# A second read moved beside the scores, one weight conversion held back, one weight split moved up

## The chip, the cores and the metric

The kernel runs on one core of one Trainium2 chip. The core has five engines that run their own instruction lists and wait for each other by semaphores: TensorE (PE in the profile), VectorE (DVE), ScalarE (ACT), GpSimd (POOL) and SyncE (SP). The metric is the device time of one execution in microseconds (us); the kernel before took 1189.47 us (median of three runs, 1189.44 to 1190.18).

## The reference, cut to what matters

Eight batches of 512 tokens and 32 state rows, 8 heads of width 64. Each token attends to the 32 state rows of its head (the first read), each state row attends to the 512 tokens (the second read, `sread`), and the 8 x 544 rows of width 512 go through two feed-forward blocks:

```python
scores = scale * x @ state^T           # per batch and head: 512 x 32
xread  = softmax(scores) @ state       # 512 x 64
scores2 = scale * state @ x^T          # 32 x 512
sread  = softmax(scores2) @ x          # 32 x 64
t = concat(xread, sread)               # 8*544 rows x 512
h = relu(t @ w_in) ** 2                # d_ff 2048
t = h @ w_out                          # 512
y = ((t @ w1) * (t @ w2)) @ w3 @ w_out2
```

## The kernel before, in words

Products run in a split form: an operand is kept as a high and a low half (`split`: ScalarE casts the high half, VectorE subtracts it to get the low one), and three passes, high x high, low x high and high x low, add up in one PSUM bank.

The first feed-forward block is cut into chunks `c` (a batch of 512 tokens) and blocks `f` of 128 hidden units. `h_tile(c, f)` is 6 matmuls of 128x512 into a bank `ph` (L535): the attention weights `aT` times `sw`, which is state times `w_in` (`make_sw`, L486). ScalarE then takes the relu (L513), the square (L515) and the high half (L519), VectorE the low half `ghl` (L520). `y_tile(c, f)` is 12 matmuls with `w_out`'s block `wo` (L580). The main loop walks a list of pairs (c, f) with an index i: 0 to 15 are blocks 0 to 7 of chunks 0 and 1 in turns of four, 16 to 23 blocks 0 to 7 of chunk 2, then 24 to 31, 32 to 39 and 40 to 47 are blocks 8 to 15 of chunks 0, 1 and 2, and so on. The `y_tile` of a step stands two steps behind its `h_tile`. Below, h9 is the `h_tile` of i = 9, and y7 the `y_tile` of the pair of i = 7.

Everything else is put beside the main loop by tables: `side[i]`, `late[i]`, `behind_y[i]`, `with_sw[i]`. A job in `side[i]` is ordered behind a gate, mostly `done[i - 3]`, the low half of the h three steps back. Inside an engine a scheduler sets the order when the program is built; on the chip each engine works off its list strictly in that order. So an instruction that waits holds up all behind it on its engine.

The jobs that matter here:

- `conv` converts one 128x512 piece of a weight that comes as 64-bit words. On VectorE that is L150, L162, L163, L164 and L167, one behind the other, into a buffer `cw` (two of these). Pieces of `w_out` are then stored by a GpSimd DMA to `w_scr` in memory (L200) and split into `wo` (L91, L92); the split is kept open (`open_splits`) until the next `conv`, or until the `y_tile` that needs it, calls `close_splits`. A third conversion needs the first one's `cw` buffer, and so waits at its L162 until the store of it has landed.
- `sread` of a batch is 64 matmuls with 128x32 tiles into a bank `ps_r` (L434); for chunk 1 (`sr1`) VectorE then copies it out to `sr` (L441). `sread_T` (`srt1`, L447) transposes `sr`.
- `scores` of a batch (`sc2` for chunk 2) is 16 matmuls with 64x32 tiles (L345), eight into each of two banks, in turns: first bank, second bank, first bank. ScalarE copies both out as `S` (L353).
- `soft1a` is the first part of a softmax on VectorE (L374, L382, L383).
- `sw_group` computes the `sw` of two groups of four blocks, 32 matmuls, and splits the four banks (L91, L92). It stands behind the `h_tile` of i = 15, 23, 31, 39 and on. The second group's banks come from the pool `bank_h`, which the next `h_tile` needs too.

`sread` and `scores` both take their banks from the pool `bank_m`, which has two:

```python
def bank_m(name):
    return psum.tile([P, 512], F32, tag="m", bufs=2, name=name)
```

The pool hands them out in turn: the bank two requests ago is handed out again once its readers are through.

Of the kernel before, what the change touches and what calls it, by code (L numbers as in the profile page):

```python
# [20 lines left out]
def kernel(  # L21
# [59 lines left out]
    def bank_m(name):  # L81
        return psum.tile([P, 512], F32, tag="m", bufs=2, name=name)

    def bank_h(name):
        return psum.tile([P, 512], F32, tag="h", bufs=2, name=name)
# [4 lines left out]
    def split(hi, lo, src):  # L90
        nc.scalar.copy(hi, src)  # L91
        return nc.vector.tensor_tensor(out=lo, in0=src, in1=f32(hi), op=ALU.subtract)  # L92
# [374 lines left out]
    def st_of(b):  # L467
        return st_pair[0][:, b - PAIR[0]] if st_pair else stT[:, b]


    def keep_warm(n):
        ps = bank_h("idle")
        for _ in range(n):
            nc.tensor.matmul(ps[:, :P], ident, ident, start=True, stop=True)

    def make_sw(b, fg, cols=slice(0, 512), banks=None, between=0, whole=False):
        pss = [banks(r, "ps_sw") if banks else bank_m("ps_sw") for r in range(G)]
        mm = None
        for k in range(HG)[::-1 if whole else 1]:
            if between and k == HG // 2:  # L480
                with tc.issue_after(mm.ins):
                    keep_warm(between)
            for r in range(G):
                rows = slice(r * D, (r + 1) * D)
                with tc.issue_after(mm.ins) if whole and mm else nullcontext():
                    mm = nc.tensor.matmul(  # L486
                        pss[r][k * NS:(k + 1) * NS, cols], st_of(b)[rows, k, :], win_t[fg][rows, k, cols],
                        start=True, stop=True, tile_position=(r * D, k * NS),
                    )
        last_sw.append(mm)  # L490
        for r in range(G):
            if (b, fg, r) not in SW:
                SW[b, fg, r] = pa.tile([P, 2, 512], F32R, tag=f"sw{r}", bufs=2, name=f"sw{r}")
            t = SW[b, fg, r]
            last = split(t[:, HI, cols], t[:, LO, cols], pss[r][:, cols])
        return last

    g_t = {}
    done = []
# [27 lines left out]
    def h_tile(c, f, hold=False):  # L527
        ph = bank_h(f"ph{c}_{f}_")
        if c < B:
            fg, m = f // 4, f % 4  # L530
            k = 0
            for g in range(G):
                s, a = SW[c, fg, g], aT_t[c, g]
                for wi, ai in PASSES:
                    mm = nc.tensor.matmul(  # L535
                        ph, s[:, wi, m * P:(m + 1) * P], a[:, ai, :],
                        start=(k == 0), stop=(k == 3 * G - 1),
                    )
                    k += 1
            h_mms.append(mm)  # L540
            act_h(c, f, ph, 512, hold=hold)
        else:
            cols = slice((f % 4) * P, (f % 4 + 1) * P)
            t = pa.tile([P, 2, ND, P], F32R, tag=f"sw{f % 2}", bufs=2, name="w9")
            split(t[:, HI], t[:, LO], win_t[f // 4][:, :, cols])
            for k in range(ND):
                wide(ph, lambda wi: t[:, wi, k, :], x9_t[k // 2][:, :, k % 2, :], k == 0, k == ND - 1)
            act_h(c, f, ph, NT9, f < 2)
# [17 lines left out]
    def y_tile(c, f):  # L566
        n = 512 if c < B else NT9
        part, (f0, f1) = [(i, sg) for i, sg in enumerate(segs[c]) if sg[0] <= f < sg[1]][0]
        if f == f0:
            for d in range(ND):  # L570
                y_ps[c, d] = bank_y(d, f"y{d}")
        if wo_t[f] is None:
            close_splits()
        t = g_t.pop((c, f))
        for d in range(ND):
            cols = slice(d * P, (d + 1) * P)
            if c == B:
                mm = wide(y_ps[c, d], lambda wi: wo_t[f][:, wi, cols], t[:, :, :n], f == f0, f == f1 - 1)
            for k, (wi, gi) in enumerate(PASSES if c < B else ()):
                mm = nc.tensor.matmul(  # L580
                    y_ps[c, d][:, :n], wo_t[f][:, wi, d * P:(d + 1) * P], t[:, gi, :n],
                    start=(f == f0 and k == 0), stop=(f == f1 - 1 and k == 2),
                )
            if f == f1 - 1:
                pool, tag = (pa, "yo") if d < 2 or c == B else (pa, "r") if c == PAIR[0] - 1 else (att, "yo2")
                o = pool.tile([P, 512], F32, tag=tag, bufs=2, name="yo")
                if c == B:
                    nc.scalar.copy(o[:, :n], y_ps[c, d][:, :n])
                    nc.vector.tensor_tensor(out=o[:, :n], in0=y_ps[c, d][:, n:], in1=o[:, :n], op=ALU.add)
                elif d % 2 and c > 1:  # L590
                    nc.vector.tensor_copy(o[:, :n], y_ps[c, d][:, :n])  # L591
                else:
                    nc.scalar.copy(o[:, :n], y_ps[c, d][:, :n])
                (nc.scalar if ALONE <= c < B else nc.sync).dma_start(y_scr[c][part][:, d, :], o[:, :n])
        return mm
# [52 lines left out]
    xp1, sc1, s21, s1a1, s1b1, at1, a2t1, sr1, srt1 = att_steps(1)  # L648
# [20 lines left out]
    first = at[1]()  # L669
# [36 lines left out]
    def sw_group(steps, sws):  # L706
        mm = h_mms[-1]
        for step in steps:
            with tc.issue_after(mm.ins):
                mm = step()  # L710
        while held:
            with tc.issue_after(read[-1].ins):
                held.pop()()
        for n, (b, fg) in enumerate(sws):
            with tc.issue_after(mm.ins):
                make_sw(b, fg, banks=(lambda r, name: bank_h(name)) if n else None)
                mm = last_sw[-1]

    def sw_high():
        make_sw(1, 0, banks=lambda r, name: bank_h(name), whole=True)  # L720

    side = {i: [] for i in range(NF * B)}
# [13 lines left out]
    side[6] = [conv, conv, sr, s21[0]]  # L736
    side[7] = [lambda srt=srt: srt(bank_h), s21[1]]
    side[8] = [a2t1[0], a2t1[1]]
    side[9] = [sr1]
    side[10] = []  # L740
    ends_at = NF * PAIR[0]
    behind_pair = 5
    spread = [32 + k * (ends_at - 32) // (40 - behind_pair) for k in range(40 - behind_pair)]
    for i in [*range(7, 11), *range(15, 31), *spread]:
        side[i].append(conv)
    pairs = {15: (2, 0), 23: (0, 2), 31: (1, 2), 39: (2, 2), 47: (3, 0)}
    for b in range(ALONE, PAIR[0]):
        pairs[b * NF + 7] = (b, 2)
# [2 lines left out]
    for g in range(G):  # L751
# [3 lines left out]
        side[11 + g].append(lambda g=g: load_xn(2, g))  # L755
    xp2, sc2, s22, s1a2, s1b2, at2, a2t2, sr2, srt2 = att_steps(2)
    late.update({
        10: [s1a2[0]], 11: [s1b2[0]], 12: [at2[0], s1a2[1]], 13: [s1b2[1]], 14: [at2[1]],
        15: [s22[0]], 16: [s22[1]], 18: a2t2,
    })  # L760
    with_sw = {i: [] for i in (*pairs, NF * PAIR[0] - 1)}
# [2 lines left out]

    def scores_and_sw():
        with tc.issue_after(h_mms[-1].ins):
            sc2()
        with tc.issue_after(scored[-1].ins):
            sw_low.append(make_sw(1, 1, banks=lambda r, name: bank_h(name)))

    side[10].append(scores_and_sw)
    behind_y, sw_low = {2: [sw_high], 6: [sw(0, 1)], 10: [srt1]}, []
    plan = {
# [73 lines left out]
    for i, (c, f) in enumerate(order):  # L847
        h_tile(c, f, bool(with_sw.get(i)))
        if i in with_sw:
            b, fg = pairs.get(i, (None, None))  # L850
            sw_group(with_sw[i], ((b, fg), (b, fg + 1)) if i in pairs else ((c0, 0), (c1, 0)))

        gate = done[i - 3] if i >= 8 else first
        with tc.issue_after(gate.ins):
            for job in side.get(i, ()):
                job()
        pend.append((c, f))
        while len(pend) > (1 if i in pairs else 2):
            last_y = y_tile(*pend.pop(0))
            with tc.issue_after(last_y.ins):  # L860
                for job in behind_y.pop(i, ()):
                    job()
        with ExitStack() as order_of:
            if i >= 8:
                order_of.enter_context(tc.issue_after(done[i - 3].ins))
            if i == 10:
                order_of.enter_context(tc.issue_after(sw_low[0].ins))
            if 10 <= i < 16:
                order_of.enter_context(tc.issue_after(casts[-1].ins))
            if i == max(pairs):  # L870
                order_of.enter_context(tc.issue_after(relus[-1].ins))
            for job in late.get(i, ()):
                job()
# [834 lines left out]
    for s, todo in enumerate((turns, turns[::-1])):  # L1708
# [3 lines left out]
        for m in range(QM):  # L1712
            ab9(m)
            if s == 0:
                for job in ((1, 2), (3,), (), (4, 5, 6, 7))[m]:
                    gate = left["split9" if m == QM - 1 else "times9"]
# [59 lines left out]
```

## Time and profile before

| | us |
|---|---|
| median of three runs | 1189.47 |
| profiled execution | 1190.18 |
| its span (first to last instruction) | 1188.4 |
| TensorE busy | 1177.2 (99%) |
| VectorE busy | 965.7 (81%) |
| ScalarE busy | 694.0 (58%) |
| GpSimd busy | 192.6 (16%) |

The span is what the profile's times count in; 1.8 us of the profiled execution lie around it. The profiled execution is the slowest of the three runs, 0.71 us above their median. Matmuls overlap, so a row's length is a little more than the time to the next row's start: pace is read from starts.

### The profile page before, as it was taken

Reading aid. Unit: us, or ns where it says so; the run is one execution under the profiler, and the core shown is the slowest. Engines: PE = TensorE matmul, PEld = TensorE weight load, DVE = VectorE, ACT = ScalarE, POOL = GpSimd, SP = SyncE. Lnnn points to the kernel's source line nnn. Section 1 sums busy time; section 2 is a strip of 40 time slices with the busy share of each in tenths; the row PEclk is TensorE's granted clock in tenths of the full one; section 3 lists DMA queues with packets and bytes.
Section 4 is the critical chain, followed back from the end, with each engine's and each line's share of the span. In section 5 each row is a group of like instructions: output and inputs, shape, how many; then the busy total and the mean of one; then the engine's idle time right before and its main releaser. Section 6 shows DMA issues by size and latency. Waiting matters only on the chain.

```text
span 1188.4 us, 17918 instructions
## 1 busy us (share of the span) xinstructions
PE 1177.2 (99%) x6400; PEld 951.0 (80%) x6400; DVE 965.7 (81%) x1723; ACT 694.0 (58%) x1269; POOL 192.6 (16%) x277
## 2 busy tenths in 40 slices
PE   7999999999999999999999999999999999999998
PEld 5677777777787777777888888888888888888888
DVE  6989787778798665677878986989898968988987
ACT  6777556565476455777867653636464636364642
POOL 0000022332431110012231001020101030313030
PEclk9999999999999999999999999999999999999999
DMA  8585688737876843447697686663524382666576
GB/s 254 125 247 198 156 258 230 188 119 180 172 192 190 182 165 121 115 111 111 98 200 251 217 205 147 106 154 65 136 69 109 137 235 62 161 98 160 88 126 177
DMA packets 204722, 187.58 MB, mean 158 GB/s; under 512 B 120648, under 2 KB 156232, under 8 KB 204104
## 3 DMA queue, kind: packets, MB, share of 16 engines
q1 hardware_dynamic: 155848, 111.70, 33.6%
q0 software_dynamic: 46768, 71.32, 28.9%
q10 hardware_dynamic: 2016, 3.41, 0.8%
q8 instruction: 50, 0.82, 0.3%
q14 instruction: 40, 0.33, 0.1%
HBM read 122.81 MB, written 82.44 MB: 173 GB/s over the span
## 4 chain that ended last, share of the span: by engine, by line
PE 93%; DVE 2%; DMA 2%; issue 1%; SPq 1%; ACT 1%; POOL 0%; DVEq 0%; POOLq 0%
PE y L580 20%; PE qa L1340 11%; PE qd L1340 7%; PE oa L1564 5%; PE ps_w L1144 4%; PE qc L1340 4%; PE qe L1340 4%; PE od L1564 3%; PE qa L977 3%; PE ps_sw L486 2%; PE ab L1419 2%; PE qd L977 2%; PE oc L1564 2%; PE oe L1564 2%; PE y L552 1%
## 5 line engine op out<-in xcount | busy, mean ns | idle before, releaser
L580 PE MATMUL y<-ghl,wo 128*128 128x512 f32 x1152 | 278.9, 392 | 0.2
L580 PEld LDWEIGHTS y<-ghl,wo 128*128 128x128 f32 x1152 | 214.7, 188 | 56.2 <-issue 10.9
L1340 PE MATMUL qa<-yq,wq 128*128 128x512 f32 x576 | 142.8, 389 | 0.0
L1349 ACT COPY s<-qa 128x512 f32<-128x512 f32 x96 | 56.5, 589 | 144.5 <-PE qa L1340 144.5
L520 DVE TENSOR_TENSOR ghl<-r,ghl 128x512 fp32r<-128x512 f32 (+1 forms) x112 | 72.5, 648 | 67.7 <-ACT ghl L519 61.6
L1340 PEld LDWEIGHTS qa<-yq,wq 128*128 128x128 f32 x576 | 108.1, 188 | 22.3
L1340 PE MATMUL qd<-yq,wq 128*128 128x512 f32 x384 | 97.4, 389 | 0.0
L1340 PEld LDWEIGHTS qd<-yq,wq 128*128 128x128 f32 x384 | 72.1, 188 | 14.9
L515 ACT ACTIVATE r<-r 128x512 f32<-128x512 f32 (+1 forms) x112 | 67.6, 603 | 3.4 <-DVE yo L591 0.7
L1249 DVE TENSOR_TENSOR yq<-yraw,yq 128x512 fp32r<-128x512 f32 x98 | 64.3, 685 | 6.0 <-ACT yq L1248 5.8
L519 ACT CAST ghl<-r 128x512 fp32r<-128x512 f32 (+1 forms) x112 | 66.3, 592 | 2.3
L1248 ACT CAST yq<-yraw 128x512 fp32r<-128x512 f32 x98 | 57.1, 622 | 6.2 <-DVE yraw L1254 3.5
L1514 POOL DMA_DIRECT2D osum<-turned x32 | 20.9, 657 | 183.4 <-DVE turned L1511 183.1
L1353 DVE TENSOR_TENSOR s<-qa,s 128x512 f32<-128x512 f32 x32 | 22.1, 689 | 33.2 <-ACT s L1349 33.1
L1340 PE MATMUL qe<-yq,wq 128*128 128x512 f32 x192 | 48.7, 389 | 0.0
L1340 PE MATMUL qc<-yq,wq 128*128 128x512 f32 x192 | 48.7, 389 | 0.0
L1144 PE MATMUL ps_w<-wo,w3T 128*128 128x512 f32 x192 | 44.1, 390 | 0.0
L1282 ACT CAST z<-q 128x512 fp32r<-128x512 f32 x64 | 37.3, 621 | 11.2 <-PE od L1575 5.3
L1287 DVE TENSOR_TENSOR q<-q,q 128x512 f32<-128x512 f32 x64 | 43.1, 683 | 0.1
L239 POOL DMA_DIRECT2D raw<-in_moe_w_dram x64 | 35.5, 598 | 46.5 <-DVE cw L167 24.8
L1340 PEld LDWEIGHTS qe<-yq,wq 128*128 128x128 f32 x192 | 36.0, 188 | 7.5
L1340 PEld LDWEIGHTS qc<-yq,wq 128*128 128x128 f32 x192 | 36.0, 188 | 7.5
(730 smaller groups left out, 2598.5 us busy)
## 6 DMA issues: line engine op xcount, KB each, us to landing
yraw<-yscr SPq DMA_DIRECT2D x56, 256.0 KB, 5.2
raw<-in_moe_w_out_dram SPq DMA_DIRECT2D x16, 512.0 KB, 4.6
yscr<-yo SPq DMA_DIRECT2D x32, 256.0 KB, 2.8
raw<-in_moe_w_dram POOLq DMA_DIRECT2D x64, 128.0 KB, 3.5
raw<-in_moe_w_dram POOLq DMA_DIRECT2D x16, 512.0 KB, 7.1
raw<-in_moe_w_in_dram SPq DMA_DIRECT2D x12, 512.0 KB, 4.4
xb<-in_x_dram SPq DMA_DIRECT2D x96, 64.0 KB, 3.2
X<-in_x_dram SPq DMA_DIRECT2D x12, 512.0 KB, 8.2
```

The costliest lines, as they stand in the source:

```text
L515: nc.scalar.activation(r[:, :n], r[:, :n], ACTF.Square)
L519: casts.append(nc.scalar.copy(t[:, HI, :n], r[:, :n]))
L520: done.append(nc.vector.tensor_tensor(out=t[:, LO, :n], in0=r[:, :n], in1=f32(t[:, HI, :n]), op=ALU.subtract))
L580: mm = nc.tensor.matmul(y_ps[c, d][:, :n], wo_t[f][:, wi, d * P:(d + 1) * P], t[:, gi, :n], start=(f == f0 and k == 0), stop=(f == f1 - 1 ...
L977: nc.tensor.matmul(ps[d], wt[:, wi, d * P:(d + 1) * P], v[:, kt, gi, :], start=(first and kt == 0 and k == 0), stop=(last and kt == 1 and ...
L1144: mm = nc.tensor.matmul(ps, t[:, wi, (j % 4) * P:(j % 4 + 1) * P], wo2_t[j][:, vi, :], start=(j == 0 and k == 0), stop=(j == N1 - 1 and k ...
L1248: left["yq"] = nc.scalar.copy(t[:, HI], src(kt))
L1249: nc.vector.tensor_tensor(out=t[:, LO], in0=src(kt), in1=f32(t[:, HI]), op=ALU.subtract)
L1287: return nc.vector.tensor_tensor(out=t, in0=a, in1=b, op=ALU.subtract)
L1340: mm = nc.tensor.matmul(ps, W[w, kt][:, wi, m * P:(m + 1) * P], Y[v, kt][:, vi, :], start=(first and kt == 0 and k == 0), stop=(last and k ...
L1349: left["copy"] = nc.scalar.copy(t, ps)
L1564: mms.append(nc.tensor.matmul(ps[d], lhs[:, wi, d], Z[v, idx][:, vi, :], start=(first and idx == 0 and k == 0), stop=(last and idx == NB - ...
```

## The change

Three moves. The second read of chunk 1 (`sr1`) leaves `side[9]` and is now the first job of `scores_and_sw` in `side[10]`, ahead of `sc2`. The split of the last `w_out` block of the first eight (`wo7`) is closed in `late[12]` ahead of the second `soft1a`, where before `y_tile` closed it. The conversion of `side[30]` (it is that of `w_out`'s block 15) goes to `side[31]`, whose gate is now the last split of the `sw` group of that step; `side[30]` only closes open splits.

```diff
         for n, (b, fg) in enumerate(sws):
             with tc.issue_after(mm.ins):
-                make_sw(b, fg, banks=(lambda r, name: bank_h(name)) if n else None)
+                copied.append(make_sw(b, fg, banks=(lambda r, name: bank_h(name)) if n else None))
                 mm = last_sw[-1]
+
+    copied = []
...
-    side[9] = [sr1]
+    side[9] = []
     side[10] = []
...
-    for i in [*range(7, 11), *range(15, 31), *spread]:
+    for i in [*range(7, 11), *range(15, 30), 31, *spread]:
         side[i].append(conv)
+    side[30].append(close_splits)
...
-        10: [s1a2[0]], 11: [s1b2[0]], 12: [at2[0], s1a2[1]], 13: [s1b2[1]], 14: [at2[1]],
+        10: [s1a2[0]], 11: [s1b2[0]], 12: [at2[0], close_splits, s1a2[1]], 13: [s1b2[1]], 14: [at2[1]],
...
     def scores_and_sw():
         with tc.issue_after(h_mms[-1].ins):
+            mm = sr1()
+        with tc.issue_after(mm.ins):
             sc2()
...
-        gate = done[i - 3] if i >= 8 else first
+        gate = copied[-1] if i == 31 else done[i - 3] if i >= 8 else first
         with tc.issue_after(gate.ins):
             for job in side.get(i, ()):
                 job()
```

How the order of instructions moves, at the two places that the prediction speaks of. First TensorE around the second read of chunk 1: `ph_5` is h9, `y` with `wo_595` is y7, `ph_6` is h10, `ps_r` the second read (its first and last rows are in these two pieces).

```order
 L535 MATMUL ph_5__910<-aT_315,sw_811 128x512 x3
+L580 MATMUL y_782<-ghl,wo_595 128x512 x3
+L580 MATMUL y_783<-ghl,wo_595 128x512 x3
+L580 MATMUL y_784<-ghl,wo_595 128x512 x3
+L580 MATMUL y_785<-ghl,wo_595 128x512 x3
+L535 MATMUL ph_6__963<-aT_259,sw_808 128x512 x3
+L535 MATMUL ph_6__963<-aT_315,sw_811 128x512 x3
 L434 MATMUL ps_r<-X_0_151,e_834 32x64 x2
 L434 MATMUL ps_r<-X_1_156,e_834 32x64 x2
```

y7 and h10 now stand ahead of the second read. The piece where the read ends, and the scores `ps_s` and the `sw` product begin:

```order
 L434 MATMUL ps_r<-X_1_156,e_775 32x64 x2
-L580 MATMUL y_782<-ghl,wo_595 128x512 x3
-L580 MATMUL y_783<-ghl,wo_595 128x512 x3
-L580 MATMUL y_784<-ghl,wo_595 128x512 x3
-L580 MATMUL y_785<-ghl,wo_595 128x512 x3
-L535 MATMUL ph_6__998<-aT_259,sw_808 128x512 x3
-L535 MATMUL ph_6__998<-aT_315,sw_811 128x512 x3
 L345 MATMUL ps_s<-xT,stT 32x512 x8
```

The scores now follow the read with nothing between them. VectorE at the same place: `wo_923` (before `wo_958`) is the split of block 5, `wo_976` that of block 6, the rows on `cw` between them are two conversions (block 6's last two rows, then all but the first row of block 7's), and `sr<-ps_r` is the copy of the second read.

```order
+L92 TENSOR_TENSOR wo_923<-cw,wo_923 128x512
+L164 SCALAR_TENSOR_TENSOR cw<-raw,cw 128x512
+L167 ISA cw<-raw,cw 128x1024
+L162 TENSOR_SCALAR cw<-raw 128x512
+L520 TENSOR_TENSOR ghl<-r,ghl 128x512
+L163 TENSOR_SCALAR cw<-cw 128x512
+L164 SCALAR_TENSOR_TENSOR cw<-raw,cw 128x512
+L92 TENSOR_TENSOR wo_976<-cw,wo_976 128x512
+L167 ISA cw<-raw,cw 128x1024
 L441 COPY sr<-ps_r 128x128
-L164 SCALAR_TENSOR_TENSOR cw<-raw,cw 128x512
-L520 TENSOR_TENSOR ghl<-r,ghl 128x512
```

The copy stood right behind the split of block 5; now eight more instructions stand ahead of it, an L162 among them that takes a `cw` buffer. Last, VectorE around the `sw` group of i = 31. Before:

```order
L92 TENSOR_TENSOR wo_2055<-cw,wo_2055 128x512
L520 TENSOR_TENSOR ghl<-r,ghl 128x512
L167 ISA cw<-raw,cw 128x1024
L150 TENSOR_SCALAR raw<-raw 128x512
L162 TENSOR_SCALAR cw<-raw 128x512
L163 TENSOR_SCALAR cw<-cw 128x512
L164 SCALAR_TENSOR_TENSOR cw<-raw,cw 128x512
L167 ISA cw<-raw,cw 128x1024
L520 TENSOR_TENSOR ghl<-r,ghl 128x512
L92 TENSOR_TENSOR sw_1996<-ps_sw,sw_1996 128x512
```

and in the changed kernel (`wo_2055` is the split of block 15 in both):

```order
L520 TENSOR_TENSOR ghl<-r,ghl 128x512
L92 TENSOR_TENSOR sw_1987<-ps_sw,sw_1987 128x512
L92 TENSOR_TENSOR sw_1990<-ps_sw,sw_1990 128x512
L92 TENSOR_TENSOR sw_2003<-ps_sw,sw_2003 128x512
L92 TENSOR_TENSOR sw_2006<-ps_sw,sw_2006 128x512
L150 TENSOR_SCALAR raw<-raw 128x512
L162 TENSOR_SCALAR cw<-raw 128x512 x2
L163 TENSOR_SCALAR cw<-cw 128x512 x2
L164 SCALAR_TENSOR_TENSOR cw<-raw,cw 128x512 x2
L167 ISA cw<-raw,cw 128x1024 x2
L92 TENSOR_TENSOR wo_2055<-cw,wo_2055 128x512
```

The two conversions that stood ahead of the `sw` splits (block 15's and the next weight's) now stand behind them, a third (the L150 to L167 of the piece of before) behind those. GpSimd's and SyncE's lists keep their order.

## Rows read from the trace of the kernel before

**Rows 1.** Page, part 1: busy time, share of the span, instructions.

```profile
PE 1177.2 (99%) x6400; PEld 951.0 (80%) x6400; DVE 965.7 (81%) x1723; ACT 694.0 (58%) x1269; POOL 192.6 (16%) x277
```

**Rows 2.** Timeline of TensorE, h9 to y8: start, length, instruction (ph__910 h9, ph__998 h10).

```profile
69.37 1.52 PE L535 MATMUL ph__910<-aT,sw 128*128 128x512 f32 x6
70.82 1.10 PE L434 MATMUL ps_r<-X,e 128*32 128x64 f32 x64
71.86 3.01 PE L580 MATMUL y<-ghl,wo 128*128 128x512 f32 x12
74.71 1.52 PE L535 MATMUL ph__998<-aT,sw 128*128 128x512 f32 x6
76.16 1.09 PE L345 MATMUL ps_s<-xT,stT 64*32 64x512 f32 x16
...
78.21 3.02 PE L580 MATMUL y<-ghl,wo 128*128 128x512 f32 x12
```

**Rows 3.** Timeline of VectorE, same stretch; in brackets the idle time before and what ended it.

```profile
71.62 0.42 DVE L162 TENSOR_SCALAR cw<-raw 128x512 f32<-128x512 f32 x1
71.96 0.42 DVE L150 TENSOR_SCALAR raw<-raw 128x512 int32<-128x512 uint32 x1
...
73.23 0.29 DVE L441 COPY sr<-ps_r 128x128 f32<-128x128 f32 x1
...
76.90 0.44 DVE L162 TENSOR_SCALAR cw<-raw 128x512 f32<-128x512 f32 x1 [1.39 <-DMA wscr<-cw]
77.37 0.43 DVE L163 TENSOR_SCALAR cw<-cw 128x512 int32<-128x512 int32 x1
...
79.05 0.69 DVE L167 CUSTOM_DVE_ANT_0 cw<-raw,cw 128x1024 uint16<-128x1024 uint16 x1
79.65 0.68 DVE L520 TENSOR_TENSOR ghl<-r,ghl 128x512 fp32r<-128x512 f32 x1
```

**Rows 4.** Timeline of GpSimd: the issue of block 5's store to memory.

```profile
72.02 0.82 POOL L200 DMA_DIRECT2D wscr<-cw  x1 [9.44 <-DVE cw L167]
```

**Rows 5.** Line L200, 60 to 180 us: the stores of w_out blocks.

```profile
DMA to landing us min/median/max: 2.3/4.3/6.5
```

**Rows 6.** Busy time by stretch: PE, PEld, DVE, ACT, POOL, then PE's clock, DMA share, GB/s.

```profile
25.00:25.50 0.50, 0.00 (x1) 0.00 (x0) 0.50 (x2) 0.50 (x2) 0.00 (x0) 1.00 0.96 393
28.50:29.00 0.50, 0.50 (x4) 0.50 (x4) 0.50 (x2) 0.50 (x2) 0.00 (x0) 0.50 1.30 201
...
31.50:32.00 0.50, 0.50 (x16) 0.00 (x0) 0.50 (x2) 0.21 (x1) 0.00 (x0) 0.74 0.00 0
```

**Rows 7.** Timeline of TensorE, 22 to 32 us: ahead of that drop.

```profile
25.72 1.64 PE L486 MATMUL ps_sw<-win,stT 64*32 64x256 f32 x16 [0.71 <-ACT xT L338]
```

**Rows 8.** Timelines of TensorE (y10, h13, y11) and VectorE (block 7's split).

```profile
86.67 2.88 PE L580 MATMUL y<-ghl,wo 128*128 128x512 f32 x12
89.39 1.52 PE L535 MATMUL ph__1151<-aT,sw 128*128 128x512 f32 x6
90.75 3.26 PE L580 MATMUL y<-ghl,wo 128*128 128x512 f32 x12
...
91.16 0.68 DVE L92 TENSOR_TENSOR wo<-cw,wo 128x512 fp32r<-128x512 f32 x1
```

**Rows 9.** Timeline of TensorE, h32 (ph__2042) and y31.

```profile
178.86 1.65 PE L535 MATMUL ph__2042<-aT,sw 128*128 128x512 f32 x6 [0.43 <-DVE sw L92]
...
182.95 2.90 PE L580 MATMUL y<-ghl,wo 128*128 128x512 f32 x12
```

**Rows 10.** Timelines of VectorE and ScalarE at the same place.

```profile
173.94 0.47 DVE L162 TENSOR_SCALAR cw<-raw 128x512 f32<-128x512 f32 x1 [0.81 <-DMA wscr<-cw]
...
176.93 2.48 DVE L92 TENSOR_TENSOR sw<-ps_sw,sw 128x512 fp32r<-128x512 f32 x4
182.50 0.69 DVE L520 TENSOR_TENSOR ghl<-r,ghl 128x512 fp32r<-128x512 f32 x1 [3.09 <-ACT ghl L519]
...
172.75 2.04 ACT L91 CAST sw<-ps_sw 128x512 fp32r<-128x512 f32 x4
```

## The prediction

> **What bounds the kernel.** I read the page's busy times first: TensorE is busy 99% of the span [rows 1], so a microsecond counts only where TensorE stands still or runs below its clock. Then I read its timeline where the change edits the order. It is nearly gapless: h9 starts at 69.37 us, y8 at 78.21 [rows 2], and all between runs without a wait. Two places show a loss that the change aims at: y11 takes 3.26 us where y10 takes 2.88 [rows 8], and h32 waits 0.43 us for VectorE [rows 9]. What can be won is therefore well under 2 us. Last I read VectorE's timeline for each instruction that TensorE will now wait for: there the change can lose more than it can win.
>
> All sums stand on the profiled execution: 1190.18 us, a span of 1188.4 plus 1.8 around it, which no edit touches. It lies 0.71 above the median of the runs, 1189.47. About 0.2% (2.4 us) is what a measurement of this kernel can tell from no change.
>
> **The second read beside the scores.** What goes: the read (64 matmuls, 1.10 us) is taken out from between h9 and y7. Undisturbed, an h tile takes 1.36 us to the next start (89.39 to 90.75) and a y tile 2.72 (86.67 to 89.39) [rows 8]. Ahead of the read h9 takes 1.45 (69.37 to 70.82), and behind it y7 takes 2.85 (71.86 to 74.71) [rows 2]. One change of tile shape less saves 0.09 + 0.13 = 0.22 us.
>
> What comes: scores and read now stand next to each other, and both take banks from a pool of two. The read takes one; the scores' first bank is the other one, their second is the read's again. So the second of the 16 score matmuls waits until VectorE has copied the read out (L441). Before, y7 and h10 (5.4 us) lay between, and the copy at 73.23 was long done at 76.16 [rows 2, 3]. TensorE takes its matmuls in order, so everything behind waits as well: the rest of the scores, `sw`, y8.
>
> When does the copy come? In the new order eight instructions stand between it and block 5's split, and the third is block 7's L162, which takes a `cw` buffer. That wait is in the trace: at 76.90 the same L162 had stood 1.39 us for the store of block 5 [rows 3], issued at 72.02 [rows 4]. Nothing that leads to this store is moved, so I keep 76.90. From there: L162 to the next independent instruction 0.34 (71.62 to 71.96), then the low half of h9, 0.60 as the equally large L167 (79.05 to 79.65), so L163 starts at 77.84 instead of 77.37, 0.47 later; what stood between L163 and 79.65 stays the same (L163, L164, block 6's split, L167) and ends at 80.12; the copy takes 0.29 [rows 3]: 80.41, some 0.04 more to TensorE, 80.45.
>
> And when does TensorE arrive? h9 at 69.37, plus 1.36 for it, 2.72 for y7 and 1.45 for h10 [rows 2, 8], puts the read at 74.90; it takes 1.04 to the next start (70.82 to 71.86) [rows 2]: scores at 75.94, the second of them at 75.99. Stall: 80.45 - 75.99 = **4.46 us**. Bounds: the stores of this line land 2.3 to 6.5 us after issue, this one 4.8 [rows 3 to 5]. At 2.3 the L162 would not wait at all: VectorE would reach it at 74.43 (it starts the L164 of block 6 at 73.23 in the copy's old place, and two rows of 0.60 follow), the copy would end at 77.94, the stall would be 2.0. At 6.5 it is 6.1. I take 4.46, since the store itself is in the trace.
>
> The Trainium skill (DMA: Bandwidth & Descriptors, Anatomy of one DMA) gives a GpSimd DMA some 2 us fixed plus its bytes at 436 GB/s. For this 256 KB store that is an estimate of 2.6 us, and by it the stall would be 2.2 us instead of 4.46. The trace does not agree for this store: 4.8 us [rows 3, 4].
>
> **The clock after the stall.** TensorE's clock is granted at its upper level (2.4 GHz) nearly all the time. In one stretch it was not: TensorE stood 0.71 us from 25.0, then ran 1.64 us of products on part of the array [rows 7]; the clock was still full at 25.0, was at half (1.2 GHz) by 28.5, and came back within the half microsecond from 31.5 [rows 6]. At half clock for 3.2 us, up to 1.6 us of work is lost. The changed kernel has a longer stretch of the same kind: read (part of the array), 4.46 us of nothing, scores and `sw` (part of the array again), 7.6 us in all. I expect the clock to fall once. If it falls as late after the halt began as it did there (25.0 to 28.5), that is near 79.5; one microsecond of the slow stretch then lies in the stall, and the other 2.2 to 2.4 cost half of themselves, **1.2 us**. Bounds: 0 (it does not fall, or all in the stall) and 2.8 (two such stretches, less what lies in the stall).
>
> **Block 7's split ahead of the softmax.** VectorE makes the low half for y11 at 91.16, behind the softmax's L383 and done at 91.84; y11 loses 3.26 - 2.88 = 0.38 [rows 8]. Now it comes one row of 0.60 earlier and is done at 91.24. But in the new order y11 needs it at its second matmul (90.75 + 2.72 / 12 = 90.98), where before four matmuls on the high half stood ahead. It still waits 0.26, so the gain is **0.1** (bounds 0 and 0.38). The stall upstream does not help: the low half of h11, which waits for ScalarE, lies between and sets VectorE back in step with TensorE.
>
> **The conversion behind the copies of the second group.** Before, VectorE stood 0.81 us for a `cw` buffer (L162 at 173.94) and worked off conversions until 176.93, only then the four `sw` splits, though ScalarE had the first high half soon after 172.75 [rows 10]. h32 needs a bank that the third split frees: it waits 0.43, and its row is 1.65 instead of 1.52 [rows 8, 9]. In the new order the splits run right behind ScalarE's casts, done by about 175.9 (2.48 for four [rows 10], from the first cast's end near 173.4): the wait goes, 0.43 + 0.13 = **0.56 us** won. What is late next: two conversions and block 15's split now stand behind them. By the same spacings (0.34, then two each of 0.34, 0.34, 0.60, 0.60, then 0.60) the split ends near 180.6; y31 needs it at 182.95 - 0.56 = 182.4 [rows 9]. The work falls into a gap of 3.09 us that VectorE had before 182.50 [rows 10]. Then a third conversion waits for block 15's store, now issued near 179.4; with 4.3 us to landing h32's low half (behind it) is ready near 185.3, and y32, some 4 us behind y31, needs it near 186.5; at 6.5 us [rows 5] up to 0.6 us are lost. I take nothing, bounds 0 to 0.6.
>
> **Sum.** -0.22 + 4.46 + 1.2 - 0.1 - 0.56 = +4.8 us: 1195.0 against the profiled execution, **1194.3** against the median. TensorE has nowhere to win it back, being busy to the end [rows 1].
>
> **Rivals.**
> - *The stall comes, the clock does not fall:* +3.6, 1193.1. For it: one fall in a whole trace is thin evidence, and some of the slow stretch can lie in the stall. Against it: 4.46 us are six times the 0.71 that led to that fall [rows 7].
> - *Longer:* the store lands late, or the clock stays down for two such stretches: +6 to +8, some 1196.5.
> - *Not slower, because the store lands early,* at block 7's L162. At 2.3 us to landing the stall is 2.0, and without a fall of the clock the sum is 2.0 - 0.88 = +1.1, 1190.6, no change that can be measured. It decides at a sum of 2.4, a stall below 3.3, a landing before 75.7 instead of 76.9. For it: the line's other stores, half of them under 4.3 us [rows 5]. Against it: this store had 4.8 with the same neighbours. (It is the case that the Trainium skill's DMA: Bandwidth & Descriptors, Anatomy of one DMA, stands for.)
> - *The change does what it says:* the scores get a free bank, no stall, all three gains: -0.9, 1188.6, no change that can be measured. Against it: the pool of two, and a copy eight instructions late.
>
> **How the numbers follow.** Forecast (stall and one fall) 0.5, stall alone 0.24, longer 0.12, early store 0.09, as it says 0.05. 1194.3 is the likeliest. The range takes the second case whole and the nearer part of the third and fourth: 1191.3 to 1196.8. Slower by over 0.2% (above 1191.9) gathers the first three, 0.86; the last two are within 0.2%, 0.13 with what they leave to the other side; faster 0.01.
>
> **What would show it.** Right: a TensorE wait of 4 to 5 us at L345 for VectorE's L441, VectorE idle about 2.4 us at L162 for the store just before; one more dip of the clock near 80 us; no wait at h32; y11 short of 3.2. Wrong: the scores run through (my reading of the banks is off), or the L162 does not wait (the store landed early). A new wait at y32 would show the third conversion's store as a cost.

## The result, and the profile after

The changed kernel takes 1196.06 us (median of 6 runs, 1195.05 to 1196.44); the kernel before, run beside it, 1189.2 (6 runs, 1188.74 to 1190.18). The ratio is 1.0056, with an interval of 1.0043 to 1.0069: slower by about half a per cent, as forecast (1194.3, range 1191.3 to 1196.8), and 1.8 us beyond the likeliest value. The profiled execution took 1195.83 us, with a span of 1194.0 against 1188.4: +5.6.

Page of the changed kernel, part 1 (busy time, share, instructions). TensorE is still busy 99% of the span, and its busy time grew by 3.1 us with the same 6400 instructions [rows 1]: a first sign that matmuls ran slower, though, as the sum below shows, not all of it is that.

```profile
PE 1180.3 (99%) x6400; PEld 952.2 (80%) x6400; DVE 965.2 (81%) x1723; ACT 694.0 (58%) x1269; POOL 192.2 (16%) x277
```

The view of waits of TensorE in the changed kernel (line waiting, line waited for: us in total, times, longest) has a first line that the kernel before does not have:

```profile
PE ps_s L345 <- DVE sr L441: 3.4, 1, 3.4
```

The timeline of TensorE at this place, changed kernel, answers to [rows 2] (ph__910 is h9, ph__963 is h10, the first `y` is y7, the second y8; in brackets the idle time before and what ended it):

```profile
68.91 1.52 PE L535 MATMUL ph__910<-aT,sw 128*128 128x512 f32 x6
70.27 2.88 PE L580 MATMUL y<-ghl,wo 128*128 128x512 f32 x12
72.99 1.52 PE L535 MATMUL ph__963<-aT,sw 128*128 128x512 f32 x6
74.44 1.10 PE L434 MATMUL ps_r<-X,e 128*32 128x64 f32 x64
75.47 1.04 PE L345 MATMUL ps_s<-xT,stT 64*32 64x512 f32 x2
79.90 1.10 PE L345 MATMUL ps_s<-xT,stT 64*32 64x512 f32 x7 [3.39 <-DVE sr L441]
...
80.81 2.76 PE L486 MATMUL ps_sw<-win,stT 64*32 64x512 f32 x15
83.49 3.79 PE L580 MATMUL y<-ghl,wo 128*128 128x512 f32 x12
```

The sum can be read off the starts. From h9 to the scores it is 6.56 us, before 6.79: one change of tile shape less, -0.23. From the scores' first matmul to the resumption it is 4.43; less some 0.05 for the step from one product to the next, the halt costs 4.38 (the 3.39 in brackets count only from the modelled end of the matmul before, so 1.0 us of the halt counts as busy; it is a third of the 3.1 us by which the busy time grew). The row x2 also sets a count right: a product of the scores is issued as two matmuls, both of the first product's ran, and what waits is the second of eight products, the third matmul and not the second of 16. From there to the end of y8 (87.28) it is 7.38, before 5.02 (76.21 to 81.23): +2.36 for the same matmuls. Together +6.51 at this place.

VectorE's timeline at the same place, changed kernel, shows why the copy is late. It answers to [rows 3]:

```profile
73.50 0.69 DVE L167 CUSTOM_DVE_ANT_0 cw<-raw,cw 128x1024 uint16<-128x1024 uint16 x1
76.35 0.43 DVE L162 TENSOR_SCALAR cw<-raw 128x512 f32<-128x512 f32 x1 [2.15 <-DMA wscr<-cw]
76.69 0.69 DVE L520 TENSOR_TENSOR ghl<-r,ghl 128x512 fp32r<-128x512 f32 x1
77.29 0.42 DVE L163 TENSOR_SCALAR cw<-cw 128x512 int32<-128x512 int32 x1
77.75 0.69 DVE L164 SCALAR_TENSOR_TENSOR cw<-raw,cw 128x512 int32<-128x512 int32 x1
78.36 0.68 DVE L92 TENSOR_TENSOR wo<-cw,wo 128x512 fp32r<-128x512 f32 x1
78.96 0.68 DVE L167 CUSTOM_DVE_ANT_0 cw<-raw,cw 128x1024 uint16<-128x1024 uint16 x1
79.56 0.28 DVE L441 COPY sr<-ps_r 128x128 f32<-128x128 f32 x1
```

VectorE stands 2.15 us for a store to memory, then works off what was queued, and only then copies the read out. The store was issued at 71.58 (GpSimd's timeline, answering to [rows 4]) and released L162 4.75 us later, at 76.33:

```profile
71.58 0.81 POOL L200 DMA_DIRECT2D wscr<-cw  x1 [9.45 <-DVE cw L167]
```

The busy view by half microseconds of the changed kernel (columns as in [rows 6]: the clock is the third number from the end) shows where the +2.36 came from:

```profile
75.00:75.50 0.50, 0.50 (x41) 0.41 (x30) 0.00 (x0) 0.50 (x2) 0.03 (x1) 1.00 1.16 434
...
77.50:78.00 0.50, 0.00 (x0) 0.00 (x0) 0.47 (x2) 0.22 (x1) 0.00 (x0) 1.00 1.07 389
78.00:78.50 0.50, 0.00 (x0) 0.00 (x0) 0.50 (x2) 0.00 (x0) 0.00 (x0) 0.84 1.02 250
78.50:79.00 0.50, 0.00 (x0) 0.00 (x0) 0.50 (x2) 0.00 (x0) 0.00 (x0) 0.50 1.22 242
...
85.00:85.50 0.50, 0.50 (x3) 0.43 (x2) 0.50 (x2) 0.00 (x0) 0.00 (x0) 0.83 0.40 139
```

All rows left out of the last gap read 0.50, that is 1.2 GHz. The clock fell near 78.3 (0.84 in that row is 0.16 us at half), still in the halt, and came back near 85.2: 6.8 us at the lower level, 5.3 of them behind the halt. The first row belongs to the store: DMA was as good as fully busy (1.16) for the second half of the time that it was under way.

The other two places. y11 on TensorE, and block 7's split and the softmax's L383 on VectorE, changed kernel, answering to [rows 8]:

```profile
96.80 0.39 PE L580 MATMUL y<-ghl,wo 128*128 128x512 f32 x1
97.35 2.79 PE L580 MATMUL y<-ghl,wo 128*128 128x512 f32 x11 [0.16 <-DVE wo L92]
...
96.61 0.69 DVE L92 TENSOR_TENSOR wo<-cw,wo 128x512 fp32r<-128x512 f32 x1
97.21 0.68 DVE L383 TENSOR_TENSOR e<-e,mx 128x512 f32<-128x512 f32 x1
```

The split now stands ahead of the softmax, and yet y11 takes 3.34 us to its end (97.35 + 2.79 - 96.80), 0.08 more than before. Then h32 and y31 on TensorE, changed kernel, answering to [rows 9]; and block 15's split with the third conversion on VectorE:

```profile
184.41 1.52 PE L535 MATMUL ph__2042<-aT,sw 128*128 128x512 f32 x6
...
188.37 2.90 PE L580 MATMUL y<-ghl,wo 128*128 128x512 f32 x12
...
186.26 0.69 DVE L92 TENSOR_TENSOR wo<-cw,wo 128x512 fp32r<-128x512 f32 x1
188.28 0.51 DVE L162 TENSOR_SCALAR cw<-raw 128x512 f32<-128x512 f32 x1 [1.33 <-DMA wscr<-cw]
```

h32 has no wait any more, y31 finds its split made 1.4 us ahead, and VectorE's new wait of 1.33 us reaches no matmul: y32 starts at 192.47, 4.10 behind y31, as before (182.95 and 187.05). y11 starts 6.05 us later than before and y31 5.42; with the 0.08 at y11, h32 has won 0.71.

One difference is not from the change. In the execution profiled before, the clock was at half by 28.5 and until about 31.8 [rows 6]; in that of the changed kernel it stayed full there. It started its `sw` product at 26.18, 0.46 later than before [rows 7], and still had h9 at 68.91, 0.46 earlier. So the span's +5.6 is -0.46 ahead of h9, +6.51, +0.08, -0.71, and some 0.2 over the rest.

### The profile page after: what moved, and what is told of

It is laid out like the page before. It is cut to its first block, busy times and chain, and to the rows that moved or that the text cites. A ratio compares the mean times of both kernels' runs of the same rounds, so it can differ in the third digit from the quotient of the medians.

```text
span 1194.0 us, 17917 instructions
## 1 busy us (share of the span) xinstructions
PE 1180.3 (99%) x6400; PEld 952.2 (80%) x6400; DVE 965.2 (81%) x1723; ACT 694.0 (58%) x1269; POOL 192.2 (16%) x277
## 4 chain that ended last, share of the span: by engine, by line
PE 92%; DVE 3%; DMA 2%; SPq 1%; ACT 1%; issue 0%; DVEq 0%
PE y L580 20%; PE qa L1345 11%; PE qd L1345 7%; PE oa L1569 5%; PE ps_w L1149 4%; PE qc L1345 4%; PE qe L1345 4%; PE od L1569 3%; PE qa L982 3%; PE ps_sw L486 2%; PE ab L1424 2%; PE qd L982 2%; PE oc L1569 2%; PE oe L1569 2%; PE y L552 1%; PE po L1457 1%
## 5 line engine op out<-in xcount | busy, mean ns | idle before, releaser
L92 DVE TENSOR_TENSOR sw<-ps_sw,sw 128x512 fp32r<-128x512 f32 (+1 forms) x66 | 40.7, 661 | 4.0 <-ACT sw L91 3.8
```

## Experiments

All kernels compute the whole reference; "idle" matmuls are additional ones whose results nothing uses. Diffs are against the changed kernel unless it says otherwise. Ratios are to the kernel before, run beside it on the same chip.

**Everything but the read's move** tells whether one of the three moves makes the whole loss.

```diff
-    side[9] = []
+    side[9] = [sr1]
...
-            mm = sr1()
-        with tc.issue_after(mm.ins):
             sc2()
```

> The second read goes back to its old place (ahead of y7); the other two moves stay. Theory: the whole loss is the scores' wait for the copy of the read and the slow clock behind it. Then this kernel has neither (no TensorE wait at L345 for L441, full clock from 70 to 90 us), h32 starts without a wait, and it takes 0.4 to 0.8 us less than the kernel before, 1188.4 to 1188.8. Rival: the conversion or the split that are still moved cost something of their own; then it stays above 1190.

Measured: 1189.15 us (10 runs, 1188.25 to 1190.16), ratio 0.9992 (0.9983 to 1.0001): 0.6 us less than the 1189.74 of the kernel before beside it, as expected, but within the interval of no difference. No wait for L441 stands at L345, and h32 starts without one. On TensorE y11 waits as in the changed kernel, so that loss belongs to the earlier split and not to the stall upstream:

```profile
90.36 2.81 PE L580 MATMUL y<-ghl,wo 128*128 128x512 f32 x11 [0.16 <-DVE wo L92]
```

**The read's move alone**, against the kernel before:

```diff
-    side[9] = [sr1]
+    side[9] = []
...
         with tc.issue_after(h_mms[-1].ins):
+            mm = sr1()
+        with tc.issue_after(mm.ins):
             sc2()
```

> The kernel before with the second read moved beside the scores and nothing else. Theory: the full loss and none of the gain at h32, 6 to 7 us over the kernel before (1195.2 to 1196.5): a wait of 3.4 to 4.5 us at L345 and a stretch of half clock. Rival: the moves need each other (the copy is late only because the other two changed VectorE's list); then this kernel is within 1 us of the kernel before.

Measured: 1195.64 us (4 runs, 1195.52 to 1199.56), ratio 1.006 (1.0039 to 1.008). TensorE has the same wait, and the clock was at half for 6.8 us, from about 79.3 to 86.1:

```profile
80.18 1.10 PE L345 MATMUL ps_s<-xT,stT 64*32 64x512 f32 x7 [3.45 <-DVE sr L441]
```

Together the two runs show that the read's new place makes the loss, and the other two moves make next to nothing.

**The copy on ScalarE** takes the copy out of VectorE's queue and leaves the order on TensorE as it is.

```diff
-            read.append((nc.scalar.copy if b >= BLK else nc.vector.tensor_copy)(t, ps[:, 0:G * D]))
+            read.append((nc.scalar.copy if b >= 1 else nc.vector.tensor_copy)(t, ps[:, 0:G * D]))
```

> The changed kernel, with the copy of the second read of chunk 1 (L441) made by ScalarE, whose list has the copy behind the relu and the square of h10. Theory: VectorE still waits some 2 us at block 7's L162 for the store, but no longer holds the copy: the scores wait about 1 us for ScalarE instead of 4.4, the clock stays full, and the kernel takes about 1189.5 (0 to 1 us over the kernel before), 6 under the changed kernel. Rival: the slow clock comes from the long run of products on part of the array, not from the halt; then the clock falls here too and 1.5 to 2.4 us stay lost (about 1191.5).

Measured: 1190.24 us (10 runs, 1189.63 to 1192.92), ratio 1.0008 (0.9999 to 1.0017). ScalarE makes the copy at 77.34, behind its own queue; the scores begin at 75.86, so 1.73 us of halt are left where some 1 was expected, and the clock stays full from 70 to 90 us. VectorE still stands 2.39 us for the store at its L162. TensorE, then ScalarE:

```profile
77.64 0.66 PE L345 MATMUL ps_s<-xT,stT 64*32 64x512 f32 x7 [0.74 <-ACT sr L441]
...
77.34 0.25 ACT L441 COPY sr<-ps_r 128x128 f32<-128x128 f32 x1
```

The next product still waits for the bank, now until ScalarE's copy is through at 77.59. The long run of part-array products (read, scores, `sw`) is in this kernel too, and in this profile it does not bring the clock down.

**No store ahead of the L162** leaves out block 5's store at this place and makes it later, so that L162 finds its buffer free.

```diff
-        if f >= 4:
+        if f >= 4 and f != 5:
             nc.gpsimd.dma_start(w_scr[:, f // 2, f % 2], w)
...
-    for f in range(4):
+    for f in (0, 1, 2, 3, 5):
```

> The changed kernel, but block 5 of w_out isn't stored from its conversion buffer; it is saved later from its split, as blocks 0 to 3 are. Block 7's L162 then has a free buffer. Theory: VectorE does not wait there, the copy of the read ends about 2.2 to 2.4 us earlier, the scores wait for it about 2 us from their first matmul instead of 4.4, and with so short a halt the clock stays full, as it did with the 1.7 us of the run with ScalarE's copy; the kernel takes 1190 to 1191. Rival: the clock falls here too (a halt of 2 us is enough), and 1.5 us more are lost: 1192 to 1193.

Measured: 1190.97 us (10 runs, 1190.32 to 1191.66), ratio 1.0008 (0.9999 to 1.0017). VectorE, then TensorE:

```profile
73.75 0.42 DVE L162 TENSOR_SCALAR cw<-raw 128x512 f32<-128x512 f32 x1
...
77.51 0.28 DVE L441 COPY sr<-ps_r 128x128 f32<-128x128 f32 x1
...
77.85 0.66 PE L345 MATMUL ps_s<-xT,stT 64*32 64x512 f32 x7 [0.98 <-DVE sr L441]
```

L162 no longer waits, and the halt is 1.97 us (75.83 to 77.85, less 0.05). So of 4.38 us some 2.4 are the store and 2.0 are VectorE's queue alone. This is the 2.0 that the prediction had as its lower bound for a store that lands early, and the clock does not fall there.

**Idle matmuls in the halt** were to separate the halt's price from the clock's: TensorE is kept busy while it waits, so that only the wait's own length is left.

```diff
         with tc.issue_after(mm.ins):
+            keep_warm(32)
             sc2()
```

> The changed kernel with 32 products of 128x128 on the identity (L474, results unused) between the second read and the scores, about 4 us of work, inside the halt. Theory: the scores start as late as in the changed kernel (the copy's end sets it), but the clock stays at its upper level, and the scores, the sw product and y8 take 4.9 us instead of 7.2: 2.4 us less than the changed kernel, about 1193.6. Rival: the 7.2 us come from something else than the clock (the operands, the banks), then it stays at 1196; or the clock falls all the same.

Measured: 1197.1 us (4 runs, 1196.34 to 1199.06), ratio 1.0063 (1.0048 to 1.0078). A miss in size: each of these products is two matmuls, the 64 took 7.41 us and outlasted the halt. The clock stayed full. So once more with 18 products, 36 matmuls:

```diff
         with tc.issue_after(mm.ins):
+            keep_warm(18)
             sc2()
```

> As the run with 32 products on the identity, whose 64 matmuls took 7.4 us and so outlasted the halt, with 18 (36 matmuls, about 4.2 us, inside the halt). Theory: the scores' second matmul still waits until VectorE's copy is through, near 79.9 us, the clock stays full, and from there to the transpose of the read (L447) it takes 4.9 us instead of 7.2: 2.3 us less than the changed kernel, about 1193.7. Rival: the copy's wait decides nothing and the time stays at 1196.

Measured: 1192.99 us (9 runs, 1192.62 to 1193.46), ratio 1.0025 (1.0015 to 1.0034). TensorE's timeline:

```profile
75.85 4.29 PE L474 MATMUL idle<-ident 128*128 128x128 f32 x36
80.07 1.19 PE L345 MATMUL ps_s<-xT,stT 64*32 64x512 f32 x16
...
82.04 3.04 PE L580 MATMUL y<-ghl,wo 128*128 128x512 f32 x12
```

The scores begin 5.25 us behind the read (5.46 to the resumption in the changed kernel), the clock is full throughout, and from the scores to the end of y8 it takes 5.01 us where the changed kernel took 7.38. The clock's price in that profile was therefore 2.4 us, and the 4.2 us ahead of the scores stayed.

**Whole-array work behind the halt.** My theory of the 6.8 us was that the part-array products behind the halt hold the clock down. Here 16 idle whole-array products stand between the scores and `sw`:

```diff
         with tc.issue_after(scored[-1].ins):
+            keep_warm(16)
             sw_low.append(make_sw(1, 1, banks=lambda r, name: bank_h(name)))
```

> The changed kernel with 16 products on the identity (32 matmuls on the whole array, 3.7 us at full clock) between the scores and the sw product; its time says nothing, its clock does. The changed kernel's clock fell near 78.1 and came back at 85.2, 7 us later, with the scores and the sw product (parts of the array) in between; the fall of the kernel before lasted 3.3 us. Theory: the clock comes back only behind work on the whole array, so with whole-array work right behind the scores it comes back earlier, 3 to 5 us after its fall. Rival: the length goes by the length of the halt; then it is 7 us again.

Measured, one run: 1198.53 us. The clock was at half for 3.4 us, in the stretch of the idle products:

```profile
80.50:81.00 0.50, 0.50 (x4) 0.50 (x5) 0.00 (x0) 0.44 (x1) 0.00 (x0) 0.74 1.19 281
...
84.00:84.50 0.50, 0.50 (x6) 0.50 (x6) 0.00 (x0) 0.00 (x0) 0.00 (x0) 0.85 0.91 348
```

That agreed with the theory, but the fall came later here, at 80.7, behind the halt's end at 79.39, so the length could have another reason. The same kernel (no further edit) was timed, together with the changed kernel itself, unedited, for a second profile.

> The changed kernel with 16 idle whole-array products (5.4 us) between the scores and sw, now timed, to settle whether the work behind the halt sets how long the clock stays at half. The halt (about 4.4 us) stays. Theory: the clock falls in every execution and comes back behind whole-array work, so the slow stretch is one of 3.2 to 3.6 us wherever it begins, not 7: mean granted clock of the executions 0.998 to 0.999 (half of 3.4 us is 0.14% of the span, 0.27% with the dip at 28 us that some executions have); in the profile one half-clock stretch of at most 4 us at place A. Rival (the length is settled by the halt or by chance, not by what runs behind): 6.8 to 7.0 us in the profile, mean clocks of 0.996 to 0.997 as in the changed kernel's own executions. Time about 1196.1 + 4.0 for the full-speed part of the idle products, about 1199 to 1201 by the theory, 1200 to 1202 by the rival; the clock tells them apart, not the time.

Measured: 1199.48 us (4 runs, 1198.66 to 1200.91), ratio 1.0083 (1.0066 to 1.0101). The profile has one stretch of 3.4 us again (81.2 to 84.7), but the mean clocks of the four executions are 0.999, 0.999, 0.996 and 0.996: in two of them the clock was down for longer in all. Where, a mean does not tell: the dip at 28 us and the end of the execution, where the clock was at half for up to 2.0 us behind the last matmul (in the last kernel below), count in it too.

> The changed kernel unaltered, on the same chip in the same call, for a second profile. Theory: halt of 3.4 us or more at the second score matmul for the copy behind the store, half clock of 6.8 to 7.0 us from between 78 and 81 us, scores to the state's turn (L447) near 7.2 us; mean clocks 0.996 to 0.997; 1195 to 1197 us, and by the clock's price 3 us over the kernel with 36 idle matmuls in the halt. Rival (the 7.0 us were one profile's chance): a stretch of 3.2 to 3.6 us here, scores to L447 near 6 us, and mean clocks of 0.998.

Measured: 1195.51 us (4 runs, 1194.7 to 1195.8), ratio 1.0045 (1.003 to 1.006); mean clocks 0.997, 0.997, 0.997 and 0.998. The second profile of the unaltered changed kernel (span 1192.9, clock 0.998), TensorE and then the half microseconds in which the clock fell and came back:

```profile
79.24 1.10 PE L345 MATMUL ps_s<-xT,stT 64*32 64x512 f32 x7 [3.28 <-DVE sr L441]
...
80.15 2.35 PE L486 MATMUL ps_sw<-win,stT 64*32 64x512 f32 x15
82.43 3.06 PE L580 MATMUL y<-ghl,wo 128*128 128x512 f32 x12
...
78.50:79.00 0.50, 0.00 (x0) 0.00 (x0) 0.50 (x2) 0.00 (x0) 0.00 (x0) 0.55 1.05 311
...
81.50:82.00 0.50, 0.50 (x14) 0.00 (x0) 0.00 (x0) 0.50 (x2) 0.00 (x0) 0.54 1.08 283
```

The theory falls: here the clock is down for 3.4 us only and comes back in the middle of `sw`, with nothing but part-array products since the halt. The same program has a stretch of 6.8 us in one execution and of 3.4 in another. From the resumption to the end of y8 it is 6.25 us here: +1.23 against the kernel before, where the first profile had +2.36. The size I expected (about 7.2 us from the scores to L447; it was 6.09) is missed for the same reason, and its rival holds for this profile; of the mean clocks three lie where the theory had them and one where the rival had it.

**The two good moves, with the split one step earlier still**: the first experiment's kernel, and the split closed in `late[11]`.

```diff
-        10: [s1a2[0]], 11: [s1b2[0]], 12: [at2[0], close_splits, s1a2[1]], 13: [s1b2[1]], 14: [at2[1]],
+        10: [s1a2[0]], 11: [close_splits, s1b2[0]], 12: [at2[0], s1a2[1]], 13: [s1b2[1]], 14: [at2[1]],
```

> The read in its old place, the conversion behind the copies of the second group as in the changed kernel, and block 7's split closed one step earlier still (in the list of i = 11, ahead of the second half of the first softmax). Theory: no wait at the scores, y11 no longer waits (2.72 us to the next start instead of 3.09 before and 3.2 in the changed kernel), h32 no longer waits: 0.9 to 1.0 us less than the kernel before. Rival: the earlier split delays the softmax and with it a later wait; then the gain is under 0.5.

Measured: 1189.4 us (11 runs, 1188.33 to 1189.62) beside 1190.04 for the kernel before (26 runs), ratio 0.999 (0.9981 to 0.9999). y11 runs through:

```profile
90.67 2.88 PE L580 MATMUL y<-ghl,wo 128*128 128x512 f32 x12
```

It takes 0.6 us less than the kernel before, not the 0.9 to 1.0 expected, and the interval barely tells that from nothing; from the first experiment's kernel (ratio 0.9992) the runs do not tell it apart. It is ahead of the changed kernel by about 0.6%.

## Why the prediction was right, and where it was not

**The stall was right, in mechanism and size.** Two products in a row that draw on a pool of two banks, and a copy eight instructions late behind L162: the arrival of the scores, the wait for the store (4.75 us to landing, 4.8 forecast) and the end of the copy all came as worked out; the halt was 4.38 us where 4.46 were forecast. (Which of the scores' matmuls waits was miscounted, as said above; it changes the sum by less than 0.1.) The read's move alone makes the loss, and both experiments that free the copy (ScalarE, no store) bring it back to within 0.1%. The rivals of an early store and of scores that run through are out. The read with a bank of another pool, which would leave the copy late and take the wait away, was not run; that the wait is for the bank is read from the trace, where the copy ends it in every kernel that has it. The Trainium skill's rule for the store (DMA: Bandwidth & Descriptors, Anatomy of one DMA; an estimate of 2.6 us for it) does not agree with this store's 4.75 us in the changed kernel either.

**The step that failed is the size of the clock's term**: "I expect the clock to fall once", with some 3.2 us at half and 1.2 lost. It fell once, near 78.3, in the halt. But in the profile that the result came with it stayed down for 6.8 us and cost 2.36, nearly the bound of 2.8 that I had put on two such stretches; that is the clock of the rival "Longer", with its 1196.5. In the second profile the stretch was 3.4 us and the cost 1.23, as in the sum. So one number was taken for a quantity that differs between executions. Which stretch is usual isn't shown. The mean clock is 0.996 to 0.997 in the six executions of the result and 0.997 to 0.998 in the four later ones, against 0.999 to 1.000 in most of the kernel before, but it also counts the dip at 28 us and the end of the execution: 0.997 can be a stretch of 6.8 us, or one of 3.4 and the dip. The kernel with 36 idle matmuls, whose clock stays up, has a ratio of 1.0025 where the changed kernel has 1.0056 and 1.0045. That is 2.4 to 3.7 us, of which the shorter wait makes 0.2, and so speaks for more than the 1.2 of the sum, with intervals of over 1 us on each. By that the 0.12 that I had given "Longer" was too low; by how much, no run shows.

That the clock would fall at all was right, for a weak reason. I had read the fall at 28 us as led to by the 0.71 us in which TensorE stood. Two more waits (0.16 and 0.36 us) follow up to that fall, and the same three, to 0.03 us, stand in all twelve traces here, while the clock falls there in six. Halts of 1.73 and 1.97 us brought no fall; the halt of some 4.4 us has one in it or behind it in all five traces that have the halt. So the forecast of one fall held, but not by "six times the 0.71".

**y11's gain of 0.1 did not come.** The split was ready 0.50 us behind y11's start, as forecast (0.49). But now it is the second matmul that waits for it, and that starts at 97.35, 0.55 behind the first where an undisturbed one follows in 0.23. That is a loss of 0.32 (0.26 forecast; the matmul starts 0.05 behind the split's end). The other 0.14 come behind it: the 11 matmuls take 2.79, where 11 of an undisturbed 12 take 2.65 (2.88 less 0.23). I had reckoned from matmul to matmul and put no cost on a restart. To win the 0.4 the split has to be done before y11 begins, as in the last kernel.

**h32 was right**: no wait, won 0.71 where 0.56 were forecast, no loss at y31 and y32. The forecast took the 0.43 us that the view gives, which count from the modelled end of the matmul before; without a wait h32 starts 0.16 ahead of that end (184.41, where the `y_tile` ahead of it ends at 184.57).

**The median lies 1.8 us beyond the forecast.** By the profile the clock makes some 1.2 of it and y11 0.2, and the halt and h32 give 0.2 back. The remaining 0.6 lie between executions and are not taken apart: the sum was worked out on an execution with the dip at 28 us and carried over to a median of three runs, 1189.47, while the executions of the kernel before range from 1188.5 to above 1193 over all its runs.

What stays open is what makes the clock's stretch 3.4 us in one execution and 6.8 in the next. What runs behind the halt does not settle it. Whether the halt's length does is open: by the rows it is 3.28 to 3.37 us in the three traces with 3.4, and 3.39 and 3.45 in the two with 6.8, a difference too narrow to rest on. Shown is only that the clock stayed up at this place in both profiles with the halt filled, and in those with halts of 1.7 and 2.0 us.

## What to carry to other kernels

Before a product is moved next to another that draws on the same small pool of banks, find the copy that frees the bank in its engine's new order, and ask what the instructions ahead of it wait for: the price here was not the copy's 0.28 us but some 2.4 us for a store two conversions upstream and 2.0 for the queue ahead of the copy. The halt of some 4.4 us cost more than its length in all five traces that have it, by the clock, so a sum for such a halt has a second term with a range, not one value. And at y11 an operand half a microsecond late at the second matmul cost 0.46 us, one that came 1.09 us late at the fifth 0.38: a split moved up only in part won nothing.

## What the runs showed of the hardware

- The clock's slow stretches in these traces were either 3.4 us (at 28 us, and behind the halt with whole-array products in two traces, with part-array products in one) or 6.8 (two traces with part-array products behind the halt). None lay between, leaving aside the end of the execution, behind the last matmul.
- The dip at 28 us is not a property of the kernel. It is there in six of the twelve traces, and missing in the others, with TensorE's rows in the same order up to there. Two rows of the changed kernel's first profile, TensorE's `sw` product with the same wait as in [rows 7], and the clock where [rows 6] has 0.50:

```profile
26.18 1.64 PE L486 MATMUL ps_sw<-win,stT 64*32 64x256 f32 x16 [0.72 <-ACT xT L338]
...
29.00:30.00 1.00, 1.00 (x7) 0.78 (x6) 1.00 (x3) 1.00 (x3) 0.00 (x0) 1.00 1.02 178
```

- The moment of the fall varies as well: near 78.3, 79.3 and 78.6 us, in the halt, but 80.7 and 81.2 where idle products ran behind it, in both 1.4 us after TensorE had resumed.
- A 128x128 product of f32 is issued as two matmuls here, of 0.12 us each at the full clock (36 in 4.29, for 18 products). The scores' 16 matmuls are eight products in the same way.
